# Attention with 128-key chunks in two of eight batches: unequal key chunks, a last chunk shared by two pairs of heads

## The chip, the cores and the metric

The kernel runs on one core of one Trainium2 chip. The metric is the device time of one execution in microseconds, the median of several runs. Times inside an execution come from one profiled run, whose span is counted from its first to its last instruction. The engines are called PE (TensorE), DVE (VectorE), ACT (ScalarE), POOL (GpSimd) and SP (SyncE).

## The reference

Attention over 8 batches and 12 heads of 448 tokens with 64 channels, with one added to the softmax's denominator, and then a two-layer network on the result, whose activation is the square of the positive part.

```python
scores = scale * np.matmul(q, k.transpose(0, 1, 3, 2))
m = np.max(scores, axis=-1, keepdims=True)
e = np.exp(scores - m)
attn = e / (np.sum(e, axis=-1, keepdims=True) + np.exp(-m) + 1e-09)
attn_out = np.matmul(attn, v)
...
x = attn_out.transpose(0, 2, 1, 3).reshape(B * S, H * D)     # 3584 x 768
h = x @ w_in                                                 # 768 x 2048
r = np.maximum(h, 0.0)
out = (r * r) @ w_out                                        # 2048 x 768
```

Multiplied through by exp(m), the weights are exp(s) / (sum of exp(s) + 1), and so the kernel takes no maximum.

## The kernel before

**Units.** Heads are taken in pairs, six to a batch, one head in each half of the partitions. A unit is one pair with a range of query columns: in batch 0 the columns are cut at FIRST = 192, so units 0 to 5 are the six pairs with 192 queries and units 6 to 11 the same pairs with 256. From unit 12 on (batch 1) each unit is a pair with all 448 queries. `units` lists them, and three loops run over them: batch 0's first columns, batch 0's other columns, batch 1. A fourth loop takes three units at a time from batch 2 on. Everything stands in an order written out by hand (`manual_schedule`): each engine runs its instructions in the order in which the program names them.

**What a unit does.** The 448 keys are cut into RUN = 4 chunks of P = 112 (a chunk holds every fourth token, since tokens are loaded as "(p t)" with t = 4). `scores` (L189) multiplies k by q for each chunk, keys on the partitions, the two heads in the two halves of the PE's rows at once; `exp` (L169, ACT) turns two chunks or one, by the unit's width, into float16 in the tile `et`. `add_chunks` (L214 to L221, DVE) adds the four chunks up to one tile `es`, by way of a tile `half`. `row_sums` (L250) multiplies `es` by ones on the PE, and ACT makes the reciprocal from a logarithm and an exponential (L253, L254). `values` (L236) multiplies v by `et`, four chunks accumulated, the two heads in the two halves of the PE's columns. `normalise` (L262, L265) multiplies both into `xt`. Sums, values and normalising of a unit come one or two units after its scores.

**q and k.** In batches 0 to 2 (`ON_PE`) they are loaded in natural order, and `transposes` (L158) turns one pair on the PE into a PSUM tile `mp`; DVE copies it into `qk` (L164), for the first three pairs in two halves. Which transposes run at which unit is in `transpose_at`. The raw float32 q and k of batch 0's first three pairs are cast first (`cast`, L148 on ACT and L150 on DVE), other pairs arrive cast. The later batches use DMA transposes.

**The network.** `queue` puts the first layer's tiles (`tile_in`, L286, then `relu_squared` on DVE, L293 and L295) on a list, and `drain` takes a share of them off between a unit's steps, so that PE has work while ACT and DVE are busy. The second layer's tiles (`tile_out`, L352) follow from unit 18 on.

**Buffers and queues.** PSUM has two tiles `sp` for scores, one `xp`, three `mp`. `et` rotates over four buffers; two more, nn0 and nn1, hold natural q and k until they are transposed, and serve later as `et`. SP and ACT issue the first raw loads (L92), POOL all other loads (L81, L99, L105, L109), in the order of the program. Each POOL load waits for an earlier one, eight places ahead, to land.

Of the kernel before, what the change touches and what calls it, by code (L numbers as in the profile page):

```python
# [15 lines left out]
def kernel(  # L16
# [19 lines left out]
    ON_PE = (0, 1, 2)  # L36
    COLS = H * S // 2 + 16
# [39 lines left out]
    def load_v(b, p0, p1):  # L77
        hs = slice(2 * p0, 2 * p1)
        if b not in vns:
            vns[b] = v_pool.tile([P, H, RUN, D], FP16, name="vn")  # L80
        nc.gpsimd.dma_start(out=vns[b][:, hs], in_=v_r[b, :, hs])  # L81

    def load_natural(b, p0, p1):

        raw = b == 0 and p1 <= 3
        for n, r in (("q", q_r), ("k", k_r)):
            src = r[b, :, 2 * p0:2 * p1]
            if raw:
                if p0 == 0:
                    whole[n] = e_pool.tile([P, RUN * S], FP32, name="et")  # L90
                t = whole[n][:, p0 * 512:(p0 + 1) * 512].rearrange("p (h t d) -> p h t d", h=2, t=RUN)
                (nc.sync if n == "q" else nc.scalar).dma_start(out=t, in_=src)  # L92
            else:
                if p0 % 3 == 0 and n == "q":
                    whole["both"] = nat.tile([P, RUN * 2 * S], FP16, name=f"nn{p0 // 3}")
                w = NPAIR * RUN * D
                t = whole["both"][:, w * (n == "k"):w * (n == "k") + w].rearrange("p (h t d) -> p h t d", t=RUN, d=D)
                t = t[:, 2 * (p0 % 3):2 * (p0 % 3 + p1 - p0)]
                nc.gpsimd.dma_start(out=t, in_=src)  # L99
            for pr in range(p0, p1):  # L100
                naturals[n, b, pr] = t[:, 2 * (pr - p0):2 * (pr - p0) + 2]
# [51 lines left out]
    def transposes(b, pr):  # L153
        tp = mp_tile(FP16)
        for i, name in enumerate("qk"):
            for s in range(RUN):
                for h in range(2):
                    nc.tensor.transpose(tp[64 * h:64 * h + 64, i, P * s:P * s + P],  # L158
                                        naturals[name, b, pr][:, h, s, :], ident[0:P, 0:P])
        if b not in qks:  # L160
            qks[b] = qk_pool.tile([128, 3, COLS], FP16, name="qk")
        parts = (0, S // 2, S) if b == 0 and pr < 3 else (0, S)
        for x, y in zip(parts, parts[1:]):
            nc.vector.tensor_copy(qks[b][:, 0:2, pr * S + x:pr * S + y], tp[:, :, x:y])  # L164
# [6 lines left out]
    def chunk(et, u, c, kk):  # L171

        n = u[3]
        if n < S:
            return et[:, 0:RUN * 2 * n].rearrange("p (c h j n) -> p c h j n", c=2, h=2, j=2)[:, c, :, kk % 2, :]
        return et.rearrange("p (k x) -> p k x", k=RUN)[:, kk]

    def scores(u, et, c, only=(0, 1)):
        b, pr, q0, n = u
        qk = qks[b]  # L180
        two = [] if n == S else s_psum.tile([P, 2, 512], FP32, name="sp")
        for kk in [2 * c + x for x in only]:
            sp = s_psum.tile([P, 2, 512], FP32, name="sp") if n == S else two
            if b in ON_PE:
                o = 0 if n == S else kk % 2 * n
                for h in range(2):
                    r = slice(64 * h, 64 * h + 64)
                    x = pr * S
                    nc.tensor.matmul(sp[:, h, o:o + n], qk[r, 1, x + P * kk:x + P * kk + P],  # L189
                                     qk[r, 0, x + q0:x + q0 + n], start=True, stop=True)  # L190
            else:
                for h in range(2):
                    for odd in range(2):
                        r = slice(64 * odd, 64 * odd + 64)
                        x = (2 * pr + h) * (S // 2)
                        kx = x + kk // 2
                        which = 1
                        if kk % 2 != odd:
                            which = 2
                            kx += kk % 2  # L200
                        nc.tensor.matmul(sp[:, odd, h * (S // 2):(h + 1) * (S // 2)],  # L201
                                         qk[r, which, kx:kx + 2 * P - 1:2], qk[r, 0, x:x + S // 2],
                                         start=True, stop=True)
            if n == S:
                exp(chunk(et, u, c, kk).rearrange("p (o x) -> p o x", o=2), sp[:, :, 0:S])
        if n < S:
            exp(et[:, 0:RUN * 2 * n].rearrange("p (c h x) -> p c h x", c=2, h=2)[:, c], two[:, :, 0:2 * n])

    def add_chunks(u, et, es, half, step):
        n = u[3]  # L210
        if n == S:
            e = et.rearrange("p (k x) -> p k x", k=RUN)
            if step < 2:
                nc.vector.tensor_add((es, half[:, 0:2 * S])[step], e[:, 2 * step], e[:, 2 * step + 1])  # L214
            else:
                nc.vector.tensor_add(es, es, half[:, 0:2 * S])  # L216
        elif step == 1:
            nc.vector.tensor_add(half[:, 0:4 * n], et[:, 0:4 * n], et[:, 4 * n:8 * n])
        elif step == 2:
            f = half[:, 0:4 * n].rearrange("p (h j n) -> p h j n", h=2, j=2)  # L220
            nc.vector.tensor_add(es[:, 0:2 * n].rearrange("p (h n) -> p h n", h=2), f[:, :, 0, :], f[:, :, 1, :])  # L221
# [10 lines left out]
    def values(u, et, xp, o=0):  # L232
        b, pr, _, n = u
        for kk in range(RUN):
            for h in range(2):
                nc.tensor.matmul(xp[64 * h:64 * h + 64, o:o + n], vns[b][:, 2 * pr + h, kk, :],  # L236
                                 of_head(chunk(et, u, kk // 2, kk), u, h), start=(kk == 0), stop=(kk == RUN - 1))

    def row_sums(us, sums):

        n = us[0][3]
        m = n * len(us)
        zp = mp_tile()
        for j, (u, parts) in enumerate(zip(us, sums)):
            for x, es in enumerate(parts):
                total = es[:, 0:2 * n]
                if n < S:
                    total = total.rearrange("p (h n) -> p h n", h=2)
                for h in range(2):
                    nc.tensor.matmul(zp[64 * h:64 * h + 64, j * n:(j + 1) * n], ones, of_head(total, u, h),  # L250
# [122 lines left out]
    ones = consts.tile([P, 64], FP16)  # L373
    nc.vector.memset(ones, 1.0 / GS)
    one_b = consts.tile([128, 1], FP32)
    nc.vector.memset(one_b, 1.0 / GS)
    for pr in range(3):
        load_natural(0, pr, pr + 1)
    nc.scalar.preload_act_table_set("natural_log_exp_and_others")
# [12 lines left out]
    load_v(1, 0, 6)  # L392

# [45 lines left out]
    FIRST = 192  # L439
# [5 lines left out]
    for i, at in ((10, (1, 0)), (11, (1, 1)), (11, (1, 2)), (13, (1, 3)), (14, (1, 4)), (15, (1, 5)), (16, (2, 0)),  # L445
                  (17, (2, 1)), (17, (2, 2))):
# [8 lines left out]
    ets, ess, rcps = {}, {}, {}  # L455
# [8 lines left out]
    def begin(i):  # L464
        spare = (i - 3 * NPAIR - 3) % 6
        if i > 3 * NPAIR + 2 and spare in (1, 2):
            ets[i] = nat.tile([P, RUN * 2 * S], FP16, name=f"nn{spare - 1}")
        else:
            ets[i] = e_pool.tile([P, RUN * 2 * S], FP16, name="et")
        es = es_pool.tile([P, 2 * S], FP16, name=f"es{i % 2}")  # L470
        half = es_pool.tile([P, 1024], FP16, name="half")
        ess[i] = (es, half)
        return units[i], ets[i], es, half

    def sums(at):

        for step in (1, 2):
            add_chunks(units[at], ets[at], *ess[at], step)

    def sums_of(at):  # L480
        return row_sums(units[at:at + 2], (ess.pop(at)[0:1], ess.pop(at + 1)[0:1]))

    def values_of(at, xp):
        values(units[at], ets.pop(at), xp, at % 2 * units[at][3])
# [9 lines left out]
    for i in range(NPAIR):  # L494
        u, et, es, half = begin(i)
        mode[0] = COLS2
        scores(u, et, 0)
        if i < 2:
            scores(u, et, 1)
# [7 lines left out]
        if i:  # L507
            sums(i - 1)
        if i > 1:
            scores(u, et, 1)  # L510
        if i in (2, 4):
            xp = x_psum.tile([128, 512], FP32, name="xp")
        if i in (2, 3, 4):
            values_of(i - 2, xp)
        if i == 4:
            values_of(3, xp)
# [6 lines left out]
    for i in range(NPAIR, 2 * NPAIR):  # L523
# [5 lines left out]
        scores(u, et, 0)  # L529
        if i == NPAIR:  # L530
# [5 lines left out]
            scores(u, et, 1)  # L536
            queue(0, FIRST)
            share[0] = left() / (NPAIR + 4)
        else:
# [3 lines left out]
            scores(u, et, 1)  # L543
# [4 lines left out]
        add_chunks(u, et, es, half, 1)  # L548
        if two and i > NPAIR:
            normalise(two, xp, rcp)  # L550
        add_chunks(u, et, es, half, 2)
# [9 lines left out]
    for i in range(2 * NPAIR, 3 * NPAIR):  # L561
# [6 lines left out]
        scores(u, et, 0)  # L568
        for at in transpose_at.get(i, ()):
            transposes(*at)  # L570
        if i == 2 * NPAIR + 3:
# [4 lines left out]
        scores(u, et, 1)  # L576
        if first:
            done = units[i - 2:i]
            values(prev, ets.pop(i - 1), xp, prev[3])
            rcp = row_sums(done, (ess.pop(i - 2)[0:1], ess.pop(i - 1)[0:1]))  # L580
        else:
            done = [prev]
            rcp = row_sums(done, (ess.pop(i - 1)[0:1],))
            values(prev, ets.pop(i - 1), xp)
        drain(share[0] * 0.15)
        for step in range(3):
            add_chunks(u, et, es, half, step)
            drain(share[0] * (0.15, 0.1, 0.15)[step])
        if i == 3 * NPAIR - 1:
            run(ins, len(ins))  # L590
            rcps[i] = row_sums([u], (ess.pop(i)[0:1],))
        normalise(done, xp, rcp)
        if first:
            queue(FIRST, S - FIRST)
# [15 lines left out]
    def take_in(at):  # L610
        xp = mp_tile()
        values(units[at], ets.pop(at), xp)
# [6 lines left out]
    def sum_up(*ats):  # L619
        for at in ats:  # L620
            rcps[at] = row_sums([units[at]], (ess.pop(at)[0:1],))
# [77 lines left out]
```

The softmax here doesn't subtract the row's maximum and nothing guards it: scores larger than these inputs give would overflow.

## Time and profile before

| | us |
|---|---|
| median of 3 runs | 412.62 (412.6 to 412.68) |
| the profiled run | 412.49 |
| its span | 410.6 |

| engine | busy us | share |
|---|---|---|
| PE | 401.0 | 98% |
| DVE | 289.8 | 71% |
| ACT | 234.4 | 57% |
| POOL | 36.3 | 9% |

A busy share is the time in which at least one instruction of that engine ran. Matmuls are pipelined, so a PE that is busy need not be at its peak. The granted TensorE clock was 0.999 of full. The DMA engines moved 45.58 MB, at a mean of 111 GB/s; in the first 70 us they are busy throughout, at about 200 GB/s.

In the lines of the profile L with a number is a line of the kernel, out<-in names tiles, sizes are partitions x elements, and what stands in brackets is the idle time before an instruction and the engine and line that ended it.

### The profile page before, as it was taken

How to read it: one execution, taken by the hardware profiler on the slowest of the kernel's cores; microseconds unless marked ns; L12 is line 12 of the kernel's file. 1: busy time of each engine (PE TensorE's matmuls, PEld its weight loads, DVE VectorE, ACT ScalarE, POOL GpSimd, SP SyncE). 2: the span in 40 equal slices, each digit the busy share in tenths (PEclk: the TensorE clock that was granted, in tenths of full speed). 3: DMA queues.
4: the chain of work that ended last, by engine and by line, in shares of the span. 5: the costliest groups of instructions: out<-in, count | busy, mean ns of one | idle time of the engine just before them, and what ended most of it. 6: DMA issues, size and time to landing. Idle time of an engine off the chain costs nothing.

```text
span 410.6 us, 10685 instructions
## 1 busy us (share of the span) xinstructions
PE 401.0 (98%) x4715; PEld 259.0 (63%) x4715; DVE 289.8 (71%) x554; ACT 234.4 (57%) x312; POOL 36.3 (9%) x58
## 2 busy tenths in 40 slices
PE   7899998999999999999999999999999999999997
PEld 3577676755576666666566666667566665555664
DVE  3778896978976787777876788867876789186000
ACT  5998997667393745559383755739464663100111
POOL 7524030020000200001000030001000000000000
PEclk9999999999999999999999999999999999999999
DMA  9999999689114891499304992297102010010222
GB/s 203 197 198 197 203 202 219 127 132 219 60 42 107 135 219 25 98 183 182 100 2 114 168 179 64 77 188 124 41 2 69 11 41 2 38 40 0 78 77 78
DMA packets 75823, 45.58 MB, mean 111 GB/s; under 512 B 42560, under 2 KB 72000, under 8 KB 75456
## 3 DMA queue, kind: packets, MB, share of 16 engines
q0 software_dynamic: 28848, 22.16, 35.6%
q1 hardware_dynamic: 46208, 22.05, 23.1%
q8 instruction: 37, 0.61, 0.6%
q10 hardware_dynamic: 720, 0.69, 0.5%
q14 instruction: 10, 0.08, 0.1%
HBM read 45.69 MB, written 17.93 MB: 155 GB/s over the span
## 4 chain that ended last, share of the span: by engine, by line
PE 89%; ACT 4%; DVE 4%; DMA 1%; issue 1%
PE mp L286 24%; PE mp L352 17%; PE mp L288 11%; PE xp L286 8%; PE sp L201 6%; PE xp L352 5%; PE mp L236 5%; PE xp L288 3%; PE xp L236 3%; PE sp L189 3%; ACT et L169 3%; PE mp L250 2%; PE mp L158 1%; DMA et<-in_k_dram 1%; DVE qk L164 1%; ACT rcp L253 1%
## 5 line engine op out<-in xcount | busy, mean ns | idle before, releaser
L169 ACT ACTIVATE et<-sp 112x896 f16<-112x896 f32 (+2 forms) x144 | 125.2, 915 | 40.7 <-PE sp L201 30.6
L352 PE MATMUL mp<-wout,gs 64*128 64x384 f16 x896 | 115.2, 322 | 0.0
L286 PEld LDWEIGHTS <-win 128*64 128x64 f16 x1536 | 83.9, 110 | 45.6 <-issue 1.5
L286 PE MATMUL mp<-xt,win 128*64 128x448 f16 (+2 forms) x1200 | 107.0, 323 | 0.3 <-DVE qk L164 0.2
L293 DVE TENSOR_SCALAR rt<-mp 128x448 f16<-128x448 f32 (+2 forms) x96 | 59.7, 622 | 26.3 <-PE mp L286 13.8
L352 PEld LDWEIGHTS <-gs 64*128 64x128 f16 x1152 | 58.1, 94 | 21.1
L295 DVE TENSOR_TENSOR gs<-rt 128x448 f16<-128x448 f16 (+2 forms) x128 | 50.2, 392 | 4.4
L352 PE MATMUL xp<-wout,gs 64*128 64x384 f16 x256 | 53.1, 323 | 0.0
L253 ACT ACTIVATE rcp<-mp,one_b 128x448 f32<-128x448 f32 (+2 forms) x42 | 26.5, 630 | 41.9 <-PE mp L250 41.7
L361 ACT ACTIVATE ot<-mp 128x384 f32<-128x384 f32 (+1 forms) x16 | 7.6, 477 | 64.5 <-PE mp L288 48.2
L201 PE MATMUL sp<-qk 64*112 64x224 f16 x480 | 43.1, 258 | 0.0
L169 ACT ACTIVATE nn<-sp 112x896 f16<-112x896 f32 x48 | 41.7, 917 | 1.6
L201 PEld LDWEIGHTS <-qk 64*112 64x112 f16 x480 | 30.6, 128 | 14.2 <-issue 3.6
L286 PE MATMUL xp<-xt,win 128*64 128x448 f16 x336 | 36.5, 352 | 0.0
L288 PEld LDWEIGHTS <-gs 128*128 128x128 f16 x256 | 24.4, 98 | 15.1 <-issue 0.4
L236 PEld LDWEIGHTS <-vn 112*64 112x64 f16 x432 | 22.4, 109 | 15.4 <-issue 3.9
L288 PE MATMUL mp<-wout,gs 128*128 128x384 f16 (+1 forms) x192 | 30.3, 317 | 0.0
L214 DVE TENSOR_TENSOR es<-et 112x896 f16<-112x896 f16 x30 | 18.7, 623 | 15.8 <-ACT et L169 15.3
L254 ACT ACTIVATE rcp<-rcp 128x448 f32<-128x448 f32 (+2 forms) x48 | 27.7, 577 | 1.5
L189 PE MATMUL sp<-qk 64*112 64x448 f16 (+2 forms) x192 | 25.8, 320 | 1.4 <-ACT et L169 0.6
L216 DVE TENSOR_TENSOR es<-es,half 112x896 f16<-112x896 f16 x42 | 26.2, 623 | 1.0
L293 DVE TENSOR_SCALAR rt<-xp 128x448 f16<-128x448 f32 x32 | 19.9, 622 | 8.2 <-PE xp L286 6.7
(63 smaller groups left out, 340.0 us busy)
## 6 DMA issues: line engine op xcount, KB each, us to landing
vn<-in_v_dram POOLq DMA_DIRECT2D x7, 672.0 KB, 9.0
out_dram<-ot SPq DMA_DIRECT2D x9, 384.0 KB, 2.3
win<-in_moe_w_in_dram POOLq DMA_DIRECT2D x8, 384.0 KB, 14.2
wout<-in_moe_w_out_dram POOLq DMA_DIRECT2D x4, 768.0 KB, 18.0
stage_q<-in_q_dram POOLq DMA_DIRECT2D x4, 676.0 KB, 11.3
stage_k<-in_k_dram POOLq DMA_DIRECT2D x4, 676.0 KB, 14.7
out_dram<-ot SPq DMA_DIRECT2D x8, 288.0 KB, 9.0
out_dram<-ot SPq DMA_DIRECT2D x9, 192.0 KB, 2.7
```

The lines of the kernel that those rows point to most:

```text
L169: nc.scalar.activation(out=out_, in_=in_, func=AF.Exp, scale=scale)
L189: nc.tensor.matmul(sp[:, h, o:o + n], qk[r, 1, x + P * kk:x + P * kk + P], qk[r, 0, x + q0:x + q0 + n], start=True, stop=True)
L201: nc.tensor.matmul(sp[:, odd, h * (S // 2):(h + 1) * (S // 2)], qk[r, which, kx:kx + 2 * P - 1:2], qk[r, 0, x:x + S // 2], start=True, sto ...
L216: nc.vector.tensor_add(es, es, half[:, 0:2 * S])
L236: nc.tensor.matmul(xp[64 * h:64 * h + 64, o:o + n], vns[b][:, 2 * pr + h, kk, :], of_head(chunk(et, u, kk // 2, kk), u, h), start=(kk == 0 ...
L253: nc.scalar.activation(out=rcp[:, 0:m], in_=zp[:, 0:m], func=AF.Ln, bias=one_b)
L254: nc.scalar.activation(out=rcp[:, 0:m], in_=rcp[:, 0:m], func=AF.Exp, scale=-1.0)
L286: nc.tensor.matmul(out_[x:x + 64], lhsT[:, x:x + 64], rhs, start=start, stop=stop)
L288: nc.tensor.matmul(out_, lhsT, rhs, start=start, stop=stop)
L293: nc.vector.tensor_scalar(out=rt[:, 0:m], in0=hp[:, 0:m], scalar1=0.0, scalar2=None, op0=ALU.max)
L295: nc.vector.tensor_mul(gs[:, f0:f0 + per, t0 % RING:t0 % RING + n], r, r)
L352: nc.tensor.matmul(o[:, 0:w], g[x:x + 64], wout[x:x + 64, fb, n0:n0 + w], start=(fb == 0), stop=(fb == NFFB - 1))
```

## The change

In batches 0 and 1 (`WIDE`) the keys are cut into three chunks of 128 and a last one of 64. Two neighbouring pairs share the last chunk: the 64 keys of the even pair lie on partitions 0 to 63, those of the odd pair on 64 to 127, and one of the two units, the owner, computes it for both (odd units in the first six, even units afterwards). So the owner has four chunk tiles and the other unit three. The pieces:

- v is loaded with 128 partitions and three tokens each; its last 64 tokens go to half of the partitions by four more loads, the other half being cleared at the start, so that `values` can multiply all 128 partitions of the shared chunk. In batch 1 POOL issues these four loads; in batch 0 SP issues three and ACT one, raw, into the buffer nn0, and DVE casts them at unit 2.
- k's copy out of PSUM puts the keys back into token order (its input steps by 112 elements, its output by one), apart from q's copy. For the first pair ACT copies q out of a PSUM tile of its own.
- `wide_scores` takes keys with a step of three; for the last chunk it makes four matmuls of 64 rows by 64 columns.
- The sums add three chunks, in place; the shared chunk is summed on the PE by `row_sums`, with a matrix `halves` that has ones for one half of the partitions and zeros for the other.
- Values of the units 0 and 1 are taken together at unit 3, not at 2 and 3. Transposes of batch 1's pairs 3 to 5 and batch 2's pairs 0 and 1 come one unit earlier, and with the last of batch 1 the loads of batch 2's second half and `stage(3)`. From unit 18 on every third unit uses nn0 or nn1 as `et`.

```diff
+    WIDE = (0, 1)
+    RW = 3
+    SW = 128 * RW
...
+        if b in WIDE:
+            nc.gpsimd.dma_start(out=vns[b][:, hs, 0:RW], in_=v[b, hs, 0:SW].rearrange("h (p t) d -> p h t d", t=RW))
...
+    def load_last_v(b):
+        for j in range(2):
+            for h in range(2):
+                to, src = last_v(b, j, h)
+                if b:
+                    nc.gpsimd.dma_start(out=to, in_=src)
+                else:
+                    (nc.scalar if (j, h) == (0, 1) else nc.sync).dma_start(out=raw_v(j, h), in_=src)
...
+    def cast_last_v():
+        for j in range(2):
+            for h in range(2):
+                nc.vector.tensor_copy(last_v(0, j, h)[0], raw_v(j, h))
...
-        parts = (0, S // 2, S) if b == 0 and pr < 3 else (0, S)
-        for x, y in zip(parts, parts[1:]):
-            nc.vector.tensor_copy(qks[b][:, 0:2, pr * S + x:pr * S + y], tp[:, :, x:y])
+        nc.vector.tensor_copy(o[:, 1].rearrange("p (n s) -> p n s", s=RUN), tp[:, 1, 0:S].rearrange("p (s n) -> p n s", s=RUN))
+        if b == 0 and pr == 0:
+            nc.scalar.activation(out=o[:, 0], in_=tps[0][:, 0, 0:S], func=AF.Copy)
+        elif b == 0 and pr < 3:
+            for x, y in ((0, FIRST), (FIRST, S)):
+                nc.vector.tensor_copy(o[:, 0, x:y], tp[:, 0, x:y])
+        else:
+            nc.vector.tensor_copy(o[:, 0], tp[:, 0, 0:S])
...
+        kks = (0, 1) if c == 0 else (2, 3) if last else (2,)
...
+                    keys = slice(x + kk, x + SW, RW) if kk < RW else slice(x + SW, x + S)
+                    to = slice(0, 128) if kk < RW else slice(64 * j, 64 * j + 64)
+                    nc.tensor.matmul(sp[to, h, o:o + n], qk[r, 1, keys], qk[r, 0, x + q0:x + q0 + n],
+                                     start=True, stop=True)
...
+            if u[0] in WIDE:
+                nc.vector.tensor_add(es, (e[:, 0], es)[step], e[:, 1 + step])
...
+            parts = [(ones, total), (halves[:, u[1] % 2], last_chunk(i))] if u[0] in WIDE else [(ones[0:P], total[0:P])]
...
-    for i, at in ((10, (1, 0)), (11, (1, 1)), (11, (1, 2)), (13, (1, 3)), (14, (1, 4)), (15, (1, 5)), (16, (2, 0)),
-                  (17, (2, 1)), (17, (2, 2))):
+    for i, at in ((10, (1, 0)), (11, (1, 1)), (11, (1, 2)), (12, (1, 3)), (13, (1, 4)), (14, (1, 5)), (15, (2, 0)),
+                  (16, (2, 1)), (17, (2, 2))):
...
+        if i >= 3 * NPAIR and i % 3 == 2:
+            ets[i] = nat.tile([128, RUN * 2 * S], FP16, name=f"nn{i // 3 % 2}")
...
+        if i == 2:
+            cast_last_v()
...
-        if i == 2 * NPAIR + 3:
+        if i == 2 * NPAIR + 2:
             load_natural(2, 3, 6)
             load_v(2, 0, 6)
             stage(3)
```

## The prediction

> **What bounds the kernel now.** I read the page first (busy shares and the 40 slices), then busy time by stage, then the chain of waits, and last the timeline around the points where the chain changes engine.
>
> ```profile
> PE 401.0 (98%) x4715; PEld 259.0 (63%) x4715; DVE 289.8 (71%) x554; ACT 234.4 (57%) x312; POOL 36.3 (9%) x58
> ...
> PE   7899998999999999999999999999999999999997
> ...
> DVE  3778896978976787777876788867876789186000
> ACT  5998997667393745559383755739464663100111
> ```
>
> One slice is 10.3 us. PE looks full everywhere, but only in the first six or seven slices are DVE and ACT nearly full beside it. That is where batches 0 and 1 are done, so I split it by stage. The edges are starts of scores (L189) in the timeline: unit 6 at 17.70, unit 12 (batch 1) at 35.87, unit 18 (batch 2) at 67.52.
>
> ```profile
> 5.00:17.70 12.70, 11.69 (x190) 6.98 (x190) 9.45 (x23) 10.92 (x16) 7.78 (x11) 1.00 1.41 212
> 17.70:35.87 18.17, 16.33 (x298) 12.45 (x298) 13.71 (x28) 16.33 (x21) 5.45 (x8) 1.00 1.45 197
> 35.87:67.52 31.65, 29.49 (x463) 21.15 (x461) 28.27 (x54) 26.96 (x36) 6.83 (x9) 1.00 1.40 207
> ```
>
> After the stretch and its length come PE, PE weight loads, DVE, ACT and POOL. Three engines stand at 74 to 93% in each stage: no single one is the bound, and a wait passes from one to the next. From 70 us on PE has no idle time in any slice but the last, in an order fixed by hand. So what is won or lost before 67.52 moves the end by as much.
>
> ```profile
> 9.52 0.69 DVE qk L164 x2
> 10.21 0.48 DVE half L218
> ...
> 10.71 0.36 DVE es L221
> 11.07 0.54 DVE qk L164
> ...
> 21.43 1.54 ACT et L169 x2
> ...
> 23.23 1.03 ACT et L169
> ...
> 24.29 0.70 DVE half L218
> ...
> 25.02 0.42 DVE es L221
> ...
> 66.53 0.64 DVE es L216
> ...
> 67.21 0.40 PE mp L250 x2
> ```
>
> The chain of waits (start, us, what) goes through DVE copies at the start, ACT's exponentials and DVE's sums in the middle, and at the end of batch 1 PE waits for the last sum. Two of PE's waits, and a DVE gap that matters below, in the timeline:
>
> ```profile
> 13.22 0.63 DVE L164 COPY qk<-mp 128x896 f16<-128x896 f16 x1 [0.76 <-PE mp L158]
> ...
> 42.56 0.40 PE L189 MATMUL sp<-qk 64*112 64x448 f16 x2 [0.41 <-ACT et L169]
> ...
> 67.21 0.38 PE L250 MATMUL mp<-es,ones 112*64 112x448 f16 x2 [1.13 <-DVE es L216]
> ```
>
> **What the Trainium skill says.** *VectorE: DVE Perf Modes*, Mode 2×_1P: two elements per cycle need 16-bit operands with step ±1. The trace agrees for the plain copy: 448 elements take 386 ns and 896 take 618 (L164), 0.52 ns each; a float32 PSUM read of 448 takes 622 (L293). The new copy of k reads with a step of 112 elements; I price it at 0.62, with 0.39 as the floor. *TensorEngine Tiling (Array Packing)*, Key Properties: a change of tiling mode drains the array. In the trace 12 matmuls of L286, two at a time, take 1.14 us, so 0.42 ns a column; two score pairs of 448 should take 0.38, but scores at 45.15 are followed by transposes at 45.67: 0.14 for the switch. *TensorE: Matmul & The Clock Gate*, Part 3: row and column tiles run together. No run here shows four 64x64 tiles at once; I take one pass of n columns, at worst two. *DMA: Bandwidth & Descriptors*, Why small descriptors are slow: three cycles per packet, so an estimate of 11 cycles for 256 B against 35 for 1 KB. No run here shows such a load.
>
> **The change part by part.** Against the profiled span of 410.6 us (its run took 412.49; the three timed runs gave 412.6 to 412.68).
>
> *ACT.* Six of twelve units of batch 0 exponentiate six tiles of n columns instead of eight, and three of six in batch 1 do three instructions instead of four. From 806, 915 and 1016 ns for 768, 896 and 1024 elements the slope is 0.82 ns: a half instruction takes about 0.49 or 0.60. Saved: 3 x 0.32, 3 x 0.42, and 3 x 0.86 (their spacing in pairs), 4.8 in all. Added: q's copy of the first pair, about 0.58 like L254's 448, in a gap (ACT waits 0.76 before the second k cast), and one load issue of 0.49 ahead of the table load, hidden before 4.80.
>
> *DVE sums.* Batch 0: (0.55 + 0.36) becomes 2 x 0.36 at n = 192, 0.69 + 0.42 becomes 2 x 0.43 at 256: 6 x 0.19 + 6 x 0.25 = 2.6. Batch 1: one add of 0.62 less, 6 x 0.62 = 3.7. In-place accumulation makes the second add wait for the first, which L216 did too.
>
> *DVE copies.* One copy of 0.62 (or two of 0.39) becomes k at 0.62 and q at 0.39 (0.25 + 0.29 where it is split). Successive copies overlap by 0.07, so a pair costs 0.32 more: eleven pairs 3.5, and pair 0 gains a little because q goes to ACT. Casting the raw v: 192 elements, by L150's 440 ns for 512 about 0.25, so four take 0.75 to 1.0. The clears of vn and the new constants, some 1.3 us by the first memset's 270 ns for 256, lie in DVE's wait for the first load (until 4.46).
>
> *PE.* Scores lose half a chunk per unit on average, row sums gain one chunk, values still take four passes. Batch 1: -3 x 0.19 + 6 x 0.19 + 3 switches of 0.14 = +1.0; batch 0's second half: -3 x 0.11 + 6 x 0.11 + 0.4 = +0.7. Four slow tiles would add 0.2 per owner, 0.6 in batch 1.
>
> *Queues.* SP gets three loads, two waiting for first loads that land before 4.8; nothing else stands on SP until an output after 70 us. On POOL the load of natural q and k of batch 1 (issued at 10.94) now waits for the casts, to about 14, and holds seven loads behind it. Four 384 KB blocks of win and a v are in flight then, 1.6 MB or 8 us at 197 GB/s: no DMA gap, cost 0. Batch 2's loads and stage(3) move one unit earlier behind a transpose that does too, cost 0: wout is needed at 67.75 and lands by 61. Moved transposes: six lie between units 12 and 18 before and after. The buffer rotation (nn at every third unit from 20) keeps two of six, cost 0.
>
> Now by stage. *To 17.70*: DVE is on the chain. Pairs 1 to 5 cost 5 x 0.32 = 1.6, three sums return 0.57, casts of 0.9 fall into the gap of 0.76 shown above: **+1.2** (+0.2 if the k copy ran at 0.39, +1.8 if the gap hid nothing). *17.70 to 35.87*: two of three shorter exponentials on the chain, -0.85; the sums after unit 7 (24.29 to 25.44) lose 0.69 of 1.12; PE's +0.7 lies on it, and two longer copies at 34.6 add 0.1: **-0.7** (+0.5 if PE's own order is the limit, -1.5 if its additions hide in ACT's time). *35.87 to 67.52*: PE is idle 31.65 - 29.49 = 2.16, and each visible wait also drains the array (0.1 to 0.2 for each of five): some 2.8 lost, of which 2.4 go when ACT has 0.86 less in odd units and DVE 0.62 less in all; PE's +1.0 stays: **-1.4** (+0.4 if half the waits come back elsewhere and tiles are slow, -1.8 at best). *After*: 0. Sum **-0.9**: 412.6 becomes **411.7**.
>
> **Rivals.** *The copies win* (slower): DVE's start loss of 1.2 is carried on, because from 20 us PE can't go faster than its order. Stage two then gives 0 and stage three -0.2, PE's longer work eating 1.0 of the 1.2 returned: +1.0 to +1.8, about 414.0. For it: PE at 0.90 to 0.93 busy in both stages; against it: the waits on ACT and DVE printed above. It decides when unit 12 starts more than 1.4 late, past 37.3.
>
> *The last v of batch 1 comes late*: the big v was issued at 25.48 and took 16.4, so landed at 41.9, and L236 read it at 43.10. Now four loads of 192 rows of 256 B follow, with the same number in batch 0 and 192 more rows in each v. At the 390 packets per us of 12 to 36 us (9347 in 24), all of them at full price, 1920 packets are 4.9 us: landing 46.8, some 3 of wait, 414.7. By bytes nothing is added, by the skill's cycles about 0.7. The later start of unit 12 helps; against it speaks that the queue is limited by bytes (197 to 207 GB/s for both 512 B and 768 B writes).
>
> *Nothing is left*: relief in ACT and DVE is paid back by PE to within 0.8: 412.4. For it: the stage sums of +1.2 and -2.1 nearly cancel.
>
> That the change doesn't do what it says I exclude: the order of instructions has seven exponentials per two batch-1 units and the new adds.
>
> **How the numbers follow.** A measurement tells 0.2%, 0.83 us, from no change. The gain case gets 0.55 (own range 410.6 to 412.2; 0.46 of it beyond 0.2%), nothing left 0.16, the copies 0.20, late v 0.09. Faster 0.46, same 0.25, slower 0.29. The range from 410.4 to 413.9 leaves out the upper half of the two slow cases and a gain above 2.2.
>
> **What would show it.** k copies of 0.6 us and DVE without gaps from 8 to 18; unit 6's scores near 18.9, unit 12's at 36.2 to 36.6, unit 18's at 66.4 to 66.9; no PE wait on L216's successor before unit 18; no PE wait for the DMA of vn. It is wrong if unit 12 starts before 35.6, if the waits of 35 to 67 stay at 2 us, or if the new 64x64 scores take two passes.

## The result, and the profile after

The changed kernel takes 415.36 us (median of 4 runs, 414.65 to 415.59) against 412.61 for the kernel before on the same chip (4 runs): a ratio of 1.0065, 95% interval 1.0048 to 1.0083. The change makes the kernel slower by some 2.7 us where I forecast 0.9 faster; 415.36 also lies above the range of 410.4 to 413.9. The profiled run of the changed kernel took 415.59, with a span of 413.8 (before: 410.6).

The page after: busy time of all engines, and the slices of PE, DVE, ACT and of the granted PE clock.

```profile
PE 403.4 (97%) x4751; PEld 259.6 (63%) x4751; DVE 289.6 (70%) x569; ACT 230.7 (56%) x310; POOL 39.2 (9%) x62
...
PE   7898999999999999999999999999999999999996
...
DVE  5758887797876787867876788867876789286000
ACT  5597887949384746739464764838464673100111
...
PEclk9699999999999999999999999999999999999999
```

ACT lost 3.7 us of work, as the change means it to. The line to stop at is the last: in the second slice, 10 to 21 us, the clock granted to PE stands at 0.6 of full. Before, all 40 slices had 9 (90% or more). The stages, cut as before at the first scores of units 6, 12 and 18 (columns: stretch, length, PE, PE weight loads, DVE, ACT, POOL, clock, DMA share, GB/s):

```profile
5.00:21.82 16.82, 13.65 (x199) 8.14 (x196) 11.46 (x31) 10.88 (x18) 9.11 (x12) 0.80 1.43 203
21.82:39.81 17.99, 16.36 (x309) 12.28 (x310) 12.65 (x31) 14.86 (x20) 6.63 (x9) 1.00 1.48 197
39.81:70.48 30.67, 29.80 (x478) 21.11 (x477) 26.06 (x52) 24.76 (x33) 7.05 (x9) 1.00 1.39 208
```

| stage | before | after | difference | forecast |
|---|---|---|---|---|
| to unit 6 | 17.70 | 21.82 | +4.1 | +1.2 |
| units 6 to 11 | 18.17 | 17.99 | -0.2 | -0.7 |
| units 12 to 17 | 31.65 | 30.67 | -1.0 | -1.4 |
| from unit 18 | 343.1 | 343.3 | +0.2 | 0 |

So the gain is there in the third stage: PE's idle time fell from 2.16 to 0.87 us. The loss is all in the first. PE's timeline there, before and then after (start, us, what; in brackets the idle time and what ended it):

```profile
8.13 0.67 PE L189 MATMUL sp<-qk 64*112 64x192 f16 x8 [0.17 <-DVE qk L164]
...
9.97 0.37 PE L189 MATMUL sp<-qk 64*112 64x192 f16 x4 [0.17 <-DVE qk L164]
...
11.09 0.52 PE L236 MATMUL xp<-et,vn 112*64 112x192 f16 x8
11.66 0.37 PE L189 MATMUL sp<-qk 64*112 64x192 f16 x4
```

```profile
8.60 0.64 PE L244 MATMUL sp<-qk 64*128 64x192 f16 x10 [0.57 <-DVE qk L213]
...
10.74 0.43 PE L244 MATMUL sp<-qk 64*128 64x192 f16 x4 [0.57 <-DVE qk L213]
11.11 0.59 PE L199 MATMUL mp<-ident,nn 112*64 112x112 f16 x8
12.08 0.58 PE L199 MATMUL mp<-ident,nn 112*64 112x112 f16 x8 [0.38 <-DMA nn<-in_k_dram]
...
13.69 0.50 PE L244 MATMUL sp<-qk 64*128 64x192 f16 x4 [0.75 <-DVE qk L215]
...
14.76 0.96 PE L199 MATMUL mp<-ident,nn 112*64 112x112 f16 x16
...
16.23 1.49 PE L309 MATMUL xp<-et,vn 128*64 128x192 f16 x16
...
18.97 0.85 PE L309 MATMUL xp<-et,vn 128*64 128x192 f16 x16
```

Three things are to be read here. Ahead of the scores of units 1, 2 and 3 PE waits 0.57, 0.57 and 0.75 us for the copy of q, which stands behind the copy of k on DVE (for units 1 and 2 PE needs only q's first 192 columns); in the kernel before it waits 0.17, 0.17 and not at all. Ahead of unit 3's scores the kernel before also has the value matmuls of unit 0 (0.52 us at 11.09), which the change moves to unit 3. The natural k of pair 3 landed 8.9 us after its issue, at about 12.0, and PE waits for it (0.38); before, it took 7.2. And the same number of value matmuls, 16, takes 1.49 us at 16.23 and 0.85 at 18.97: between them the clock came back. In windows, one line of the kernel before and then the changed kernel (columns as in the stages above):

```profile
8.00:11.00 3.00, 2.71 (x49) 1.72 (x49) 2.48 (x9) 2.41 (x4) 1.68 (x3) 1.00 1.45 194
```

```profile
8.00:11.00 3.00, 1.87 (x32) 1.02 (x31) 2.52 (x9) 1.69 (x3) 0.49 (x1) 0.98 1.43 188
11.00:14.00 3.00, 1.87 (x26) 0.98 (x22) 1.70 (x6) 1.30 (x2) 1.15 (x2) 0.50 1.51 193
10.87:17.70 6.83, 5.70 (x73) 3.80 (x69) 4.95 (x15) 3.95 (x6) 3.17 (x5) 0.50 1.49 196
```

In 8 to 11 us PE is busy for 1.87 of 3 us (before, 2.71), and from 10.87 to 17.70, for 6.83 us, it gets half its clock. DVE's copies and casts, by group (busy us, mean ns):

```profile
L208 DVE COPY qk<-mp 128x448 f16<-128x448 f16 x12 | 7.5, 621 | 4.1 <-PE mp L199 4.1
L215 DVE COPY qk<-mp 128x448 f16<-128x448 f16 x9 | 3.4, 381 | 0.0
L205 DVE COPY qk<-mp 128x896 f16<-128x896 f16 x3 | 1.8, 615 | 0.0
L112 DVE CAST vn<-nn 64x192 f16<-64x192 f32 x4 | 1.2, 340 | 0.0
```

The copies are as priced, the casts 340 ns and not 250.

### The profile page after: what moved, and what is told of

It reads as the page before. It is cut to its first block, busy times and chain, and to the rows that moved or that the text cites. A ratio compares the mean times of both kernels' runs of the same rounds, so it can differ in the third digit from the quotient of the medians.

```text
span 413.8 us, 10793 instructions
## 1 busy us (share of the span) xinstructions
PE 403.4 (97%) x4751; PEld 259.6 (63%) x4751; DVE 289.6 (70%) x569; ACT 230.7 (56%) x310; POOL 39.2 (9%) x62
## 4 chain that ended last, share of the span: by engine, by line
PE 91%; ACT 3%; DVE 2%; DMA 2%; POOL 1%; issue 0%; POOLq 0%; DVEq 0%
PE mp L363 24%; PE mp L429 17%; PE mp L365 10%; PE xp L363 8%; PE sp L273 6%; PE xp L429 5%; PE mp L309 5%; PE xp L309 4%; PE xp L365 3%; PE mp L327 3%; DMA nn<-in_k_dram 2%; PE sp L244 2%; ACT et L220 2%; PE mp L199 1%; PE sp L261 1%; ACT rcp L330 1%
## 5 line engine op out<-in xcount | busy, mean ns | idle before, releaser
L220 ACT ACTIVATE et<-sp 112x896 f16<-112x896 f32 (+5 forms) x141 | 121.2, 900 | 47.8 <-PE sp L273 30.6
L309 PEld LDWEIGHTS <-vn 112*64 112x64 f16 (+1 forms) x432 | 22.9, 112 | 15.3 <-issue 2.7
L285 DVE TENSOR_TENSOR es<-et 112x896 f16<-112x896 f16 x24 | 14.9, 622 | 15.5 <-ACT et L220 15.5
L287 DVE TENSOR_TENSOR es<-es,half 112x896 f16<-112x896 f16 x36 | 22.4, 623 | 0.8
L436 DVE TENSOR_SCALAR ot<-mp 128x384 f32<-128x384 f32 x28 | 15.6, 558 | 9.6 <-PE mp L429 6.1
```

What stands on the lines that cost most here:

```text
L220: nc.scalar.activation(out=out_, in_=in_, func=AF.Exp, scale=scale)
L287: nc.vector.tensor_add(es[0:P], es[0:P], half[0:P])
L309: nc.tensor.matmul(xp[64 * h:64 * h + 64, o:o + n], vns[b][r, 2 * pr + h, kk, :], of_head(e, u, h), start=(kk == 0), stop=(kk == RUN - 1))
L436: nc.vector.tensor_scalar(out=ot[:, n0:n0 + w], in0=op[:, 0:w], scalar1=OUT_SCALE, scalar2=None, op0=ALU.mult)
```

## The experiments

Theories for the 4.1 us of the first stage: A, the four raw loads of batch 0's last v delay the natural q and k; B, DVE's copies and casts stand ahead of PE; C, PE, starved by A or B, is granted half its clock for some microseconds. Each needs something different to go away. Each version was timed beside the kernel before, whose median was 412.5 to 412.66 each time; the ratios are against that.

**The loads left out.** In batch 0 the last keys of v are zero, so they add nothing to the values.

```diff
...
-    load_last_v(0)
+    raw_v(0, 0)
+    nc.vector.memset(whole["v"][:, 0:NPAIR * D], 0.0)
```

> The four raw loads of batch 0's last v are left out and the buffer is cleared instead, so the last 64 tokens of v count as zero; the casts stay. Theory A (the 768 rows of 256 B delay the natural q and k of pair 3 from 10.3 to 12.0, PE starves, and its clock is halved from 11 to 17.4): k of pair 3 lands near 10.5, unit 6 starts near 19.5 instead of 21.82, clock 1.0 throughout, about 413.0. Theory B (DVE's longer copies and casts alone starve PE): k lands early but PE still waits for copies, the clock still falls, unit 6 later than 21, 415 or so.

Measured: 414.19 (12 runs, 413.04 to 415.16), ratio 1.0028 (1.0016 to 1.0039). PE no longer waits for a DMA, but the waits of 0.57, 0.57 and 0.74 us for copies stay, and its profiled run has the halved clock. The runs sort by the mean granted clock: 413.04 to 413.2 at 1.00 (five), 414.19 to 414.34 at 0.996 (five), 414.93 and 415.16 at 0.992. At equal clocks the loads are worth 0.3 to 0.4 us (0.996: 414.56 to 414.65 for the changed kernel). A alone is not the cause of the loss.

**One copy for q and k.** q and k leave PSUM in one plain copy of 896, with no copy on ACT and no split; the keys stay in load order, so the keys of batches 0 and 1 meet the v of other tokens.

```diff
...
-        nc.vector.tensor_copy(o[:, 1].rearrange("p (n s) -> p n s", s=RUN), tp[:, 1, 0:S].rearrange("p (s n) -> p n s", s=RUN))
...
+        nc.vector.tensor_copy(o[:, 0:2], tp[:, :, 0:S])
```

> q and k of a pair leave PSUM in one plain copy of 896 elements, as before the change, and ACT's copy is gone; k stays in the order of the load, so a query's keys are paired with other tokens' v. Theory B: the copies were the loss of the first stage, unit 6 starts near 19 to 19.5, about 413. Theory A: PE waits for the load of pair 3 until 12.0 all the same, unit 6 starts at 21 or later, 414.5 to 415.

Measured: 418.62 (4 runs, 416.6 to 420.95), ratio 1.015 (1.0102 to 1.0197), the clock between 0.984 and 1.00: slower, against both theories, and slower even in the run at 1.00 (416.6). The scores now wait for all of the copy, without the early q of 192 columns, so the run doesn't test the price of the k copy. Its trace shows a new wait in batch 1 as well:

```profile
46.81 0.56 PE L229 MATMUL sp<-qk 64*128 64x448 f16 x4 [1.84 <-DVE qk L202]
```

These scores stand behind the copy of pair 3, although unit 13 reads pair 1. One copy now spans the planes of q and k in the tile; that this is why these scores wait for it is a guess that was not tested.

**More warming.** Both kernels have a few matmuls (`keep_warm`) of a cleared tile, of which nobody reads the result: they only keep PE busy. Here nine more of them, of 128x128x512, stand in units 0 to 2, where PE waits.

```diff
+        if i == 2:
+            keep_warm(2)
...
-            keep_warm(1)
+            keep_warm(3)
...
-        if i in (1, 3, 5):
-            keep_warm(1 + i // 5)
+        if i in (1, 2, 3, 5):
+            keep_warm({1: 3, 2: 3, 3: 1, 5: 2}[i])
```

> Nine more warming matmuls of 512 columns where PE waited at units 0 to 2; nothing else. Theory C (a good part of the loss is the halved clock, which follows from the waits whatever their cause): clock 1.0 from 8 to 20, values of units 0 and 1 take 0.85 instead of 1.49, unit 6 starts near 20.4, about 414.0. If the clock is only a symptom on an idle PE: unit 6 stays at 21.8 and the time at 415.4 or above.

Measured: 413.88 (413.83 to 414.05, 6 runs), ratio 1.0032 (1.002 to 1.0043). The clock is full in all six, with windows of

```profile
8.00:11.00 3.00, 2.73 (x36) 1.19 (x34) 2.52 (x9) 1.70 (x3) 1.15 (x2) 1.00 1.42 188
11.00:14.00 3.00, 2.84 (x37) 1.25 (x35) 2.22 (x7) 1.63 (x3) 0.50 (x1) 1.00 1.50 194
```

PE has more to do, all of it of no use, and the kernel is 1.5 us faster (0.7 against the second measurement of the changed kernel below): C is shown to be a cause. Unit 6 starts at 20.18, as the theory asked (20.4). 1.2 us of loss remain.

**The casts left out.** Loads stay, the cast part of v is cleared instead.

```diff
+            if b == 0:
+                nc.vector.memset(rows[64 * j:64 * j + 64, j, :, :, RW, :], 0.0)
...
-        if i == 2:
-            cast_last_v()
```

> The four casts of batch 0's last v are left out (that part of v is cleared instead), the loads stay. Theory B with the casts as the larger part: the copy of pair 4 starts 1 us earlier, unit 6 near 20.8, about 414.3. Theory A: the casts lie in PE's slow time, and less than 0.5 is won, 415 or so.

Measured: 414.58 (413.14 to 414.64, 5 runs), ratio 1.0041 (1.0028 to 1.0054): one run at full clock with 413.14, four at 0.995 to 0.996 with 414.46 to 414.64. With the clock halved for a while the casts cost nothing that shows (the changed kernel has 414.6 at 0.996 as well). In the trace, which is of the run at full clock, unit 6 starts at 19.39.

**Last v of batch 0 through POOL.** Loaded with the cast on the way, behind the natural q and k of pairs 4 and 5; no raw buffer, no cast on DVE.

```diff
-                if b:
-                    nc.gpsimd.dma_start(out=to, in_=src)
-                else:
-                    (nc.scalar if (j, h) == (0, 1) else nc.sync).dma_start(out=raw_v(j, h), in_=src)
+                nc.gpsimd.dma_start(out=to, in_=src)
...
-    load_last_v(0)
...
     load_natural(0, 4, 6)
+    load_last_v(0)
...
-        if i == 2:
-            cast_last_v()
```

> Edit: the last keys of batch 0's v go through POOL's queue with the cast on the way, behind the natural q and k of pairs 4 and 5; no raw buffer, no DVE casts. All else as in the changed kernel. Theory A+B (the four loads on SP and ACT and the four casts are what the first part pays, 0.4 and 0.8 us by the runs so far, the halved clock another 1.4): about 412.9 where the clock stays full and 414.3 where it falls, so a median between 412.7 and 414.4. Theory D (the loads only move: with rows of 256 bytes they hold up what stands behind them on POOL's queue, or the values of units 0 and 1 wait for them): 414.5 or more, with a wait on DMA before the values of unit 0 or 1.

Measured: 414.19 (412.67 to 415.01, 20 runs), ratio 1.0029 (1.002 to 1.0039). At full clock 412.67 to 413.05 (six runs), at 0.995 and 0.996 413.79 to 414.44, at 0.992 414.53 to 415.01. PE doesn't wait for the new loads, so theory A+B holds and D doesn't. At full clock the stages, and PE's waits in the first of them, read

```profile
5.00:19.31 14.31, 11.66 (x199) 6.90 (x199) 10.05 (x28) 10.83 (x18) 10.99 (x15) 1.00 1.46 200
19.31:37.30 17.99, 16.37 (x309) 12.30 (x309) 12.65 (x31) 14.86 (x20) 6.69 (x9) 1.00 1.45 196
37.30:67.97 30.67, 29.79 (x478) 21.13 (x476) 26.06 (x52) 24.76 (x33) 7.81 (x10) 1.00 1.43 203
```

```profile
8.53 0.64 PE L241 MATMUL sp<-qk 64*128 64x192 f16 x10 [0.57 <-DVE qk L210]
...
10.68 0.35 PE L241 MATMUL sp<-qk 64*128 64x192 f16 x4 [0.57 <-DVE qk L210]
...
12.56 0.35 PE L241 MATMUL sp<-qk 64*128 64x192 f16 x4 [0.83 <-DVE qk L212]
```

Without raw loads, casts and halved clock the first stage still costs 19.31 - 17.70 = 1.6 us, and stages two and three give back 1.2: 0.4 of loss is left, as in the spans (411.0 against 410.6). The 1.6 us are idle time of PE: it is busy for 11.66 us here and 11.69 before. The three waits for the copy of q, 0.57, 0.57 and 0.83 us against 0.17, 0.17 and nothing, grew by as much (+1.63). How much of the third wait the moved value matmuls of unit 0 would have filled was not tested.

**Batch 1 alone.** Wide chunks only there; batch 0 with the copies, sums and order of the kernel before.

```diff
-    WIDE = (0, 1)
+    WIDE = (1,)
...
+            parts = (0, S // 2, S) if b == 0 and pr < 3 else (0, S)
+            for x, y in zip(parts, parts[1:]):
+                nc.vector.tensor_copy(o[:, 0:2, x:y], tp[:, :, x:y])
...
-    load_last_v(0)
```

> Edit: wide chunks in batch 1 alone; batch 0 as in the kernel before (copies in halves, half sums, values order), no load and no cast of a last v of batch 0. Theory of the split (the whole loss arises in batch 0's first part, and the third part keeps its gain of 1.0 us by itself): 411.7, range 411.3 to 412.1, unit 6 at 17.7, unit 12 at 35.9, unit 18 at 66.5, full clock. Rival (the third part only gains because its transfers or MLP work were already late or put off after a slow first part): 412.4 to 412.9.

Measured: 411.95 (411.77 to 412.66, 20 runs) against 412.58 (53 runs), ratio 0.9987 (0.998 to 0.9994), clock 0.999 to 1.00 in all: faster than the kernel before by 0.6 us. No other version was as fast. Its stages, and PE at the end of the second stage, in the kernel before and in this version:

```profile
5.00:17.81 12.81, 11.74 (x191) 7.00 (x190) 9.79 (x24) 11.04 (x16) 8.04 (x11) 1.00 1.41 212
17.81:36.38 18.57, 16.34 (x297) 12.31 (x297) 14.34 (x31) 16.33 (x21) 6.88 (x10) 1.00 1.45 197
36.38:67.03 30.65, 29.64 (x474) 21.16 (x472) 26.27 (x52) 24.66 (x33) 7.82 (x10) 1.00 1.43 203
```

```profile
35.25 0.69 PE L286 MATMUL mp<-xt,win 128*64 128x192 f16 x12
```

```profile
35.76 0.69 PE L364 MATMUL mp<-xt,win 128*64 128x192 f16 x12 [0.47 <-DVE qk L209]
```

The third stage has its 1.0 by itself, so it is no make-up for a late start. The second is 0.4 longer than before although batch 0 is as before: ahead of unit 12 PE waits 0.47 us for DVE's copies of batch 1's q, where the kernel before has no wait. This version keeps the moved transposes and loads of batches 1 and 2, so it doesn't tell the wide chunks' share of the 1.0 us from theirs.

**Through POOL, and more warming.**

> Edit: as in the run with the last v through POOL, and nine more warming products in units 0, 1 and 2. Theory A+B+C: clock 1.00 in all runs, 412.3 to 412.9, about 1.2 under the run with the warming products alone (413.88). Theory D (the loads only move their cost): 413.5 to 414.5.

Measured: 413.46 (412.78 to 413.63, 12 runs), ratio 1.0019 (1.0011 to 1.0028), clock 0.999 to 1.00. Both theories missed: 413.46 lies between their ranges. Against 412.67 to 413.05 without the warming at full clock, the nine matmuls cost 0.6 to 0.7 themselves (unit 6 at 19.97 instead of 19.31), which I had left out. They hold the clock, at a price.

**Neither loads nor casts, and more warming.**

> Edit: neither loads nor casts of batch 0's last v (that part of v cleared instead, so the last keys of batch 0 add nothing to the values), and the nine warming products. What is left of the change in the first part is the copies of q and k and the wide chunks. Theory A+B+C: 412.7 (413.88 less 0.8 and 0.4), so the copies and chunks alone give back what the third part gains. The prediction's sum for the same (copies +1.6, sums -0.57, no casts, then -0.7 and -1.4): about 410.9.

Measured: 413.55 (412.93 to 413.81, 10 runs), ratio 1.0021 (1.0012 to 1.003), full clock. Against the run with the warming alone (413.88) loads and casts together come to 0.3 us, less than the 1.2 I expected. The prediction's sum for this version is not 410.9 as I wrote: its terms, +1.6 - 0.57 - 0.7 - 1.4, make 411.5, and with the 0.6 to 0.7 of the warming 412.2. The measured time is 1.4 above that at full clock, so the clock explains none of it, nor do loads and casts. What is left in batch 0 are the copies, the sums, the moved values and the new chunks; the waits shown above point to the copies, but no run takes these apart.

**k copied on ACT.** As the version through POOL; for pairs 1 to 5 of batch 0 (in the second run pairs 1 and 2) ACT copies k.

```diff
+        if b == 0 and pr > 0:
+            nc.scalar.activation(out=k_to, in_=k_from, func=AF.Copy)
+        else:
+            nc.vector.tensor_copy(k_to, k_from)
```

> Edit: as the run with the last v through POOL, and ACT copies k of pairs 1 to 5 of batch 0, beside DVE's copy of q (0.52 us by the ACT copy of q of pair 0). Copy theory (PE starves at units 1 to 3 because the 0.62 us copy of k stands ahead of q on DVE, 0.57, 0.57 and 0.83 us of waits at full clock; the starved PE is what lets the clock fall): waits of 0.1 to 0.4 us, unit 6 at about 18.4 instead of 19.3, clock 1.00 in most runs, 411.6 to 412.2. Rival (ACT is strictly in order and the exponentials behind the copies come 0.5 us later each, six or seven times): unit 6 at 19.3 or later, 412.7 or more at full clock, and a clock that still falls.

> Edit: as the run before it, with pairs 1 and 2 alone on ACT. Copy theory: two of the three waits go, unit 6 at 18.7, 411.9 to 412.4 at full clock, and the clock falls in fewer than half of the runs. Rival: no change to the run with the last v through POOL, 412.7 at full clock and 414 to 415 otherwise.

Measured: 416.21 (415.7 to 416.7) and 416.61 (416.47 to 416.73), ratios 1.0089 (1.0073 to 1.0104) and 1.0098 (1.0083 to 1.0113), the clock at 0.988 to 0.995. The copies didn't run side by side. DVE's timeline of the first of the two:

```profile
8.57 0.46 DVE L214 COPY qk<-mp 128x192 f16<-128x192 f16 x2 [1.77 <-ACT qk L207]
...
11.25 0.46 DVE L214 COPY qk<-mp 128x192 f16<-128x192 f16 x2 [1.55 <-ACT qk L207]
```

q and k of a pair lie in one PSUM tile, and DVE's copy of q waits for ACT's copy of k; PE waits 1.09 and 1.10. The theory was not tested. That the clock is low in all eight runs fits its clock part, and shows no more, since the copies come later as well.

**k on ACT, a tile each.** The same with separate PSUM tiles for q and k, as the changed kernel has them for pair 0: first for pairs 1 to 3, then for 1 to 5.

```diff
-        if b == 0 and pr == 0:
+        if b == 0 and pr == 0 or b == 0 and pr in (1, 2, 3):
             tps = [mp_tile(FP16), tps[0]]
...
-                nc.vector.tensor_copy(o[:, 0, x:y], tp[:, 0, x:y])
...
+                nc.vector.tensor_copy(o[:, 0, x:y], tps[0][:, 0, x:y])
```

> Edit: as the run with the last v through POOL; for pairs 1 to 3 of batch 0 the transposes of q and k go to a PSUM tile each, ACT copies k (0.55 us) while DVE copies q (0.25 for the first 192 queries). Copy theory: the waits of units 1 to 3 for copies fall from 0.57, 0.57 and 0.83 us to about 0.4 each (the ACT copy alone), unit 6 at 18.5 to 18.9, the clock at 1.00 in most runs, a median of 411.9 to 412.4. Rival (ACT's order: each copy of k stands behind the exponentials of the unit before, so it ends no earlier than DVE's did): waits of 0.6 or more, 412.7 at full clock, the clock falling in most runs, a median of 414.

> Edit: as the run before it, for pairs 1 to 5. Copy theory: as the run before it or up to 0.3 us better, 411.7 to 412.4. Rival: the exponentials of units 3 to 5 come 0.5 us later behind the copies, and the third buffer of the PSUM pool is missed by the row sums: 0.3 to 1.0 us above the run before it.

Measured: 414.78 (412.66 to 415.27, 13 runs), ratio 1.0045 (1.0034 to 1.0056), and 414.5 (412.65 to 415.36, 10 runs), ratio 1.0038 (1.0024 to 1.0052). For the first version the rival holds; the second came out 0.3 us below the first, where its rival had said 0.3 to 1.0 above and the copy theory 411.7 to 412.4, so neither holds there. DVE's copies of q now wait only for PE, but PE waits for ACT, whose copy stands behind the exponentials of the unit before (ACT, then PE, of the first run):

```profile
6.92 1.19 ACT L221 ACTIVATE et<-sp 128x768 f16<-128x768 f32 x2
8.00 0.55 ACT L207 ACTIVATE qk<-mp 128x448 f16<-128x448 f16 x1
```

```profile
8.60 0.64 PE L245 MATMUL sp<-qk 64*128 64x192 f16 x10 [0.81 <-ACT qk L207]
...
10.99 0.50 PE L245 MATMUL sp<-qk 64*128 64x192 f16 x4 [0.92 <-ACT qk L207]
...
13.03 0.50 PE L245 MATMUL sp<-qk 64*128 64x192 f16 x4 [0.37 <-ACT qk L207]
```

Neither DVE nor ACT has room for the copy of k at that place. That starving by these copies sets off the clock is not shown from this side; it rests on the warming run. One of the 13 runs of the first version took 415.27 although its mean clock was 1.00 (the two others at 1.00 took 412.66 and 413.16); no trace of it was kept, so what held it up is open.

**The changed kernel again.**

> Edit: none, the changed kernel itself, to see how its time goes with the granted clock over more runs. Clock theory: most runs at 0.992 to 0.996 and 414.6 to 415.6; a run at 1.00, should there be one, at 413.2 to 413.6, which is the change without the halved clock. Rival (the clock is a companion of the loss and not its cause): a run at 1.00 within 0.5 us of the others.

Measured: 414.6 (414.56 to 415.21, 4 runs), ratio 1.0054 (1.0037 to 1.0071): three runs at 0.996, one at 0.992. Its trace has the waits for copies (0.57, 0.57 and 0.83 us) but none for a DMA, so the late natural k of pair 3 is not needed for the loss; unit 6 starts at 20.85. None of the eight runs of this kernel had the full clock. What it would take at full clock is therefore an estimate. From 1.00 to 0.996 lie 1.2 us in the version without the loads and 1.6 in the one through POOL, to 0.992 lie 1.9 and 2.0: 414.6 less 1.2 to 1.6, and 415.4 less 1.9 to 2.0, make 413.0 to 413.5.

## Why the prediction was wrong

**The step that failed is "To 17.70: +1.2".** It measured +4.1. Its terms, against the runs:

| term | priced | measured |
|---|---|---|
| copies of pairs 1 to 5 | +1.6 | +1.6 for copies, sums and all else without loads and casts |
| three sums | -0.57 | 0.13 a unit on DVE (0.81 against 0.94), not 0.19; no gain in PE's waits |
| casts of the last v | 0.9 into a gap of 0.76: +0.14 | 0.3 at full clock (413.1 without the loads, 412.8 without both) |
| raw loads on SP and ACT | 0 | 0.3 to 0.4 at equal clock |
| granted PE clock | not in the sum | 1.2 to 1.6 at 0.996, 1.9 to 2.0 at 0.992 |

**The largest missing term is the clock.** It was put at nothing, because the kernel before shows 1.00 throughout; the profiled run, at 0.992, lost some 2 of its 4.1 us to it. The Trainium skill (*TensorE: Matmul & The Clock Gate*, Part 1) says that PE's clock is gated to half after an idle window of about 3.4 us, in windows that run freely, not from the kernel's start. I used that page for its tiles alone. The traces agree with the length: where the clock is halved it is so for 3.41 us (second measurement of the changed kernel), 6.83 (the first, and five other versions) or 10.24 us (k of pairs 1 and 2 on ACT). Half the clock for 3.4 us of 412 is an estimate of 0.4% a step, and the means of the runs stand near 1.00, 0.996, 0.992, 0.988 and 0.984. The traces differ on the word idle, and they decide: PE was never idle for 3 us here. The stretches of 3.41 us just ahead of the fall, in the two measurements, and the halved stretch of the second:

```profile
7.46:10.87 3.41, 2.28 (x44) 1.22 (x38) 2.63 (x9) 2.23 (x4) 0.55 (x2) 1.00 1.42 189
```

```profile
9.98:13.39 3.41, 1.95 (x31) 1.01 (x31) 3.17 (x10) 2.05 (x4) 1.21 (x2) 1.00 1.46 193
13.39:16.81 3.42, 3.40 (x43) 2.55 (x42) 2.74 (x9) 2.46 (x4) 2.00 (x3) 0.50 1.50 196
```

In the eight traces with a fall PE was busy for 1.7 to 2.3 of these 3.41 us, and in the stretch before that one for 2.4 or more. The kernel before has 2.4 or more in every such stretch from 4 to 20 us. This suggests how one kernel can have no, one or two halved stretches: where the stretches lie differs from run to run. A low busy share does not always bring the fall, though. In the version with one copy PE was busy for 1.94 us between 43.02 and 46.43, and in the kernel before for 2.28 of the 3.41 us from 63.8, and the clock stayed. Part 4 of the same page says that transposes do not count as busy in the same way. Nothing here supports that as the reason: in 8 to 11 us transposes take 0.69 of PE's 1.87 us, and in the kernel before, at full clock, 1.31 of 2.71.

**The copies were sized well on DVE and wrongly for PE.** k takes 621 ns and q 381, as priced. But PE doesn't pay the 0.32 us that a pair costs DVE. Before, it could start on the first half of q and k (0.39 us of copy); now it needs all of k and then q's first columns (0.62 and 0.25, starting 0.54 after k): 0.40 more at units 1 and 2, and 0.83 at unit 3, with no visible cost for pairs 4 and 5. That this sums to 1.6 again is luck. The sums don't give the 0.57 back, since they stand behind these copies on DVE. The upper bound for the stage, +1.8, is about what full clock would have given: unit 6 is 1.7 late in the version with loads and without casts (19.39).

**"17.70 to 35.87: -0.7"** measured -0.2. The term that was too small is "two longer copies at 34.6 add 0.1": the version with batch 1 alone has this preparation without the rest, and its second stage is 0.4 longer. Taking that off, batch 0's own part is an estimated -0.6 against a priced -0.8.

**"35.87 to 67.52: -1.4"** measured -1.0: right in direction, with both terms too large. PE's idle time fell by 1.3 and not by 2.4, which is more than the 2.16 of idle time there was: the prediction had added 0.1 to 0.2 a wait for a draining array, and no run here takes that apart. PE's busy time rose by 0.3 and not by 1.0. The gain is there in the version with batch 1 alone too (-1.0). It lies in the waits that the prediction named, for exponentials and the last sum, but the transposes that now come one unit earlier were not tested apart. Part of the wait for the last sum before unit 18 stayed, 0.47 of 1.13:

```profile
69.98 0.38 PE L327 MATMUL mp<-es,ones 128*64 128x448 f16 x2 [0.47 <-DVE es L283]
```

**Queues, "cost 0".** On POOL this held: the load of natural q of batch 1 waited 3.7 us for the casts, and DMA shows no gap up to 70 us. On SP and ACT it did not quite, see the loads above: I asked only whether the new loads land in time, not what they take from the loads in flight beside them.

**The rivals.** "The copies win" comes nearest: its 414.0 is 0.5 to 1.0 above the estimate at full clock, and unit 12 started at 39.81, past its point of 37.3. But its mechanism (PE can't give back a start loss of 1.2) is not what happened: the later stages gave back 1.2 us (-0.2 and -1.0), and the start loss was larger. "The last v of batch 1 comes late" is false: v's first part landed at 42.0, its last piece at 43.5, and PE never waited for it. The sign "the new 64x64 scores take two passes" did not come: four 64x64 tiles with 448 columns take 0.38 us, as two 64x128 tiles do (0.37).

What stays open: what besides PE's busy time decides whether its clock stays, and whether transposes count; and in the first stage, the share of the moved value matmuls.

## What to carry to other kernels

Ahead of a place where engines hand work to each other in short turns, a forecast should price what PE loses when it is starved twice: once the wait, and once the clock that it may be granted afterwards; compare PE's busy time in stretches of about 3.4 us with that of the kernel before. Price a copy by when the waiting engine can start, and not by the time that the copying engine spends. Ask for each saving whether it stands ahead of the wait or behind it on the engine that ends the wait. And try such a change in one batch at a time: here it paid in batch 1 alone (411.95 against 412.58), where the added copies cost 0.4 us, and not in the start-up of batch 0.

## What the runs showed of the hardware

- PE's clock fell to half without any long idle time, behind 3.41 us in which PE was busy for 2.28 (changed kernel) or 1.95 (its second measurement), and came back after 6.83 or 3.41 us; in the other traces with a fall it was 6.83 or 10.24. The share of busy time alone doesn't decide: the version through POOL ran at full clock with PE busy for 1.90 of 3 us (8 to 11 us), and fell in 14 of its 20 runs.
- Warming matmuls with no use made the changed kernel 0.7 to 1.5 us faster, with the clock full in all 6 runs, and cost 0.6 to 0.7 where it was full anyway.
- ACT copies 448 columns out of PSUM with a step of 112 in 0.55 us, DVE in 0.62; DVE takes 0.38 without the step, so the step costs it 0.24.
- Four 64x64 tiles ran in one pass: 448 columns in 0.38 us.
